# First attention's value products: softmax weights stationary, four heads in four column tiles

## The chip, the cores and the metric

The kernel runs on 1 core of one Trainium2 chip. The metric is the device time of one execution in microseconds; the time before is the median of 3 runs, 1287.91 us (1282.92 to 1290.34). Engines in the profile: PE is TensorE's matmul, PEld its weight load, DVE VectorE, ACT ScalarE, POOL GpSimd, SP SyncE, which issues most DMAs.

## The reference

Three parts follow one another, all in float32 (8 batches, 8 heads, 576 tokens, head size 64, 32 packing queries):

```python
def sm_attn(qq, kk, vv):
    s = scale * np.matmul(qq, kk.transpose(0, 1, 3, 2))
    s = s - np.max(s, axis=-1, keepdims=True)
    a = np.exp(s)
    a = a / (np.sum(a, axis=-1, keepdims=True) + 1e-09)
    return np.matmul(a, vv)
p_packed = sm_attn(p, k, v)          # first attention
out = sm_attn(q, p_packed, p_packed) # second attention
...
h = np.maximum(x @ w_in, 0.0)        # first MLP, 4608 x 512 x 2048
x = h * h @ w_out
...                                  # then a top-1 MoE of 8 experts, 512 x 1024 x 512
```

The change is in the last line of the first `sm_attn`: weights (32 x 576 per head) times values (576 x 64 per head).

## The kernel before, in words

**The first attention** works in 16 quads (four heads of one batch; `quads`, L282), each a generator `att1(i)` (L283) that is advanced by one step per iteration of the loop at L888. Its steps are:

1. scores: 32 packing queries of each head against the 576 keys, four matmuls into `s1` (L297); then the load of the K of quad i+3.
2. softmax: maximum (L308), exponential with the row's sum `sm` (L310), `sm` + 1e-9 and its reciprocal (L313, L314), and the scaling of all 128 x 576 weights by it on ScalarE (L315).
3. transposes: five, into PSUM tiles `ta` and `tb` (L320, L321), copied to `aT` on ScalarE (L322) and VectorE (L323). Rows of `aT` are now keys, columns are 4 heads x 32 queries.
4. value products `pq` (L329, L330): for each pair of heads (`g`) and each of five blocks of keys (four of 128, one of 64), the values of both heads (128 columns) are the stationary operand and 64 columns of `aT` the moving one. Each fp32 matmul is recorded as two instructions. The result has head size in rows; half of it is for the wrong head and is not used. Then the load of the V of quad i+4 (`load_v`), two copies of the wanted halves into `pp32` on VectorE (L334), and the split of `pp32` into a rounded part and a rest, `pphl` (L346 ScalarE, L347 GpSimd).

Quad i does step 1 in iteration i and step 4 in iteration i+3. In an iteration the oldest quad comes first, then from the newest to the next oldest (L891). The loop has 19 iterations.

**Beside it**, in the same loop: `conv_in` turns the first MLP's float64 weights into float32 halves in `wbt` (`convert`, L198: one ScalarE square, four VectorE operations, a ScalarE copy, a GpSimd difference); `att2(0)` is the second attention's first 384 tokens, from iteration `A20` on (L225, L896); and `pw_unit(bp, u)` (L352) multiplies the packed values of two batches (pair `bp`) with `w_in`, because the kernel applies the MLP's first weight to the packed values and not to the tokens. It makes three matmuls `ph` (L361), a copy `pws` (VectorE for odd pairs, L365; ScalarE for even ones, L367) in one of three buffers, and a write to DRAM (`pw_d`, L370). The table `PW` (L221 to L224) says which units are made in which iteration; those not made there follow in `others` (L914), with `conv_out`, which turns `w_out` and overwrites `wbt[:, u]` once all four pairs have used it. Only then does the MLP start (`layer1` L463, `layer2` L489), with the second attention's other tiles beside it, and at last the MoE (`group`, L768).

**Order.** Each engine has one queue and works in order. The program's order is a priority: a planner places the instructions of all engines by a simulated timeline and may interleave single matmuls of different steps. PSUM in this loop: `s1` has two tiles of two banks; `ta`, `tb`, `pq`, `pw`, `s2` and `ta2` share four banks in turn (`bank`, L256).

Of the kernel before, what the change touches and what calls it, by code (L numbers as in the profile page):

```python
# [20 lines left out]
P = 128  # L21
# [5 lines left out]
def tile_pack_attention_moe_moe2(  # L27
# [191 lines left out]
    w_out32 = w_out64.bitcast(I32).rearrange("r (f t) -> r f t", t=2)  # L219
    NU = 4 * HP  # L220
    PW = {9 + i: [(0, 2 * i), (0, 2 * i + 1)] for i in range(4)}  # L221
    PW |= {13 + i: [(1, 2 * i), (1, 2 * i + 1)] for i in range(6)}
    for i in range(3):
        PW[16 + i].append((2, i))  # L224
    A20 = 4  # L225
    PRI = 0
    a2T = {}

# [54 lines left out]
    def att1(i):  # L283
        b, qd = quads[i]
        pb = ptb[b % 2]
        if qd == 0:
            for j in range(2):
                nc.gpsimd.tensor_copy(
                    pb[j * D : (j + 1) * D, :, j * NPK : (j + 1) * NPK], pn[j * D : (j + 1) * D, b]
                )  # L290
        kT, vv, a, aT = kbuf[i % 3], vbuf[i % 4], abuf[i % 2], atbuf[i % 2]
        vt = vv[:, :16].rearrange("p (r h) d -> p r (h d)", h=4)
        vl = vv[:LAST, 16:].rearrange("p h d -> p (h d)")
        s1 = held["early"].tile([P, 2, 512], F32, tag="s1", name="s1", bufs=2)
        for hf in range(2):
            for pr in range(2):
                nc.tensor.matmul(  # L297
                    s1[pr * 64 : (pr + 1) * 64, hf, :HS],
                    pb[:, 2 * qd + pr, :],
                    kT[:, pr, hf * HS : (hf + 1) * HS],  # L300
                    start=True,
                    stop=True,
                )
        load_k(i + 3)
        yield
        mx = a_p.tile([P, 1], F32, tag="mx", name="mx")
        sm = a_p.tile([P, 1], F32, tag="sm", name="sm")
        nc.vector.tensor_reduce(out=mx, in_=s1[:, :, :HS], axis=AX.XY, op=ALU.max)  # L308
        nc.vector.tensor_scalar(out=mx, in0=mx, scalar1=-SCALE, scalar2=None, op0=ALU.mult)
        nc.scalar.activation(  # L310
            out=a.rearrange("p (h s) -> p h s", h=2), in_=s1[:, :, :HS], func=AF.Exp, bias=mx, scale=SCALE, accum_out=sm
        )
        nc.vector.tensor_scalar(out=sm, in0=sm, scalar1=EPS, scalar2=None, op0=ALU.add)  # L313
        nc.vector.reciprocal(out=sm, in_=sm)  # L314
        nc.scalar.activation(out=a, in_=a, func=AF.Copy, scale=sm)  # L315
        yield
        ta = bank("t", "ta")
        tb = bank("t", "tb")
        for r in range(4):
            nc.tensor.transpose(ta[:, r * P : (r + 1) * P], a[:, r * P : (r + 1) * P], ident)  # L320
        nc.tensor.transpose(tb[:LAST, :P], a[:, MAIN:S], ident)  # L321
        nc.scalar.activation(out=aT[:, 0:4, :].rearrange("p r n -> p (r n)"), in_=ta, func=AF.Copy)  # L322
        nc.vector.tensor_copy(aT[:LAST, 4, :], tb[:LAST, :P])  # L323
        yield
        pq = bank("t", "pq")
        for g in range(2):
            ds, ns = slice(2 * g * D, 2 * (g + 1) * D), slice(2 * g * NPK, 2 * (g + 1) * NPK)
            for r in range(4):
                nc.tensor.matmul(pq[:, ns], vt[:, r, ds], aT[:, r, ns], start=(r == 0), stop=False)  # L329
            nc.tensor.matmul(pq[:, ns], vl[:, ds], aT[:LAST, 4, ns], start=False, stop=True)  # L330
        load_v(i + 4)
        gs = slice(2 * qd, 2 * qd + 2)
        for j in range(2):
            nc.vector.tensor_copy(  # L334
                pp32[j * D : (j + 1) * D, b, gs, j * NPK : (j + 1) * NPK],
                pq[j * D : (j + 1) * D, :P].rearrange("p (g i n) -> p g i n", g=2, i=2)[:, :, j, :],
            )
        hl = pphl[:, b // 2].rearrange("p x g (b n) -> p x g b n", b=2)
        if b < 2:
            places = [(slice(2 * qd + i, 2 * qd + i + 1), (b + i) % 2) for i in range(2)]  # L340
        else:
            places = [(gs, b % 2)]
        for g, o in places:
            src = pp32[:, b, g, :]
            hi = hl[:, 0, g, o, :]
            nc.scalar.activation(out=hi, in_=src, func=AF.Copy)  # L346
            nc.gpsimd.tensor_tensor(out=hl[:, 1, g, o, :], in0=src, in1=hi.bitcast(F32), op=ALU.subtract)  # L347
        yield
# [536 lines left out]
    held["at"] = st3.enter_context(tc.tile_pool(name="at", bufs=1, side="left"))  # L885
    cv, co = [conv_in()], []
    runs, bg = [], []
    for i in range(len(quads) + 3):  # L888
        if i < len(quads):
            runs.append(att1(i))  # L890
        for r in (runs if i < 3 else runs[:1] + runs[:0:-1]):  # L891
            with tc.high_priority(offset=PRI):
                next(r)
        if i >= 3:
            runs.pop(0)
        if i == A20:  # L896
            bg = [att2(0)]
        pull(bg)
        pull(cv, 2)
        if i == 8:  # L900
            pull(cv, NU)
            held["head"] = const.tile([P, HEAD, 2, NPC, P], F32R, tag="head", name="head")
        for bp, u in PW.get(i, ()):
            pw_unit(bp, u)
# [156 lines left out]
```

## Time and profile before

| | us |
|---|---|
| median of 3 runs | 1287.91 |
| lowest, highest | 1282.92, 1290.34 |
| the profiled execution | 1283.14 |
| its span, first to last instruction | 1281.3 |
| TensorE busy in it | 1234.5 |
| VectorE busy | 810.7 |
| ScalarE busy | 600.7 |
| GpSimd busy | 323.9 |

The rows come from the one profiled execution. A line of a group gives line, engine, operation, what it writes and reads, its form (partitions x elements) and count, then busy time and mean ns of one, then the engine's idle time before it and what ended it. A line of the timeline gives start and length in us of instructions of one kind merged, with their count; the length runs to the end of the last one, and matmuls overlap the next one's start. The chain of waits is followed back from the stretch's last instruction to what released each step.

### The profile page before, as it was taken

How to read it: one execution, taken by the hardware profiler on the slowest of the kernel's cores; microseconds unless marked ns; L12 is line 12 of the kernel's file. 1: busy time of each engine (PE TensorE's matmuls, PEld its weight loads, DVE VectorE, ACT ScalarE, POOL GpSimd, SP SyncE). 2: the span in 40 equal slices, each digit the busy share in tenths (PEclk: the TensorE clock that was granted, in tenths of full speed). 3: DMA queues.
4: the chain of work that ended last, by engine and by line, in shares of the span. 5: the costliest groups of instructions: out<-in, count | busy, mean ns of one | idle time of the engine just before them, and what ended most of it. 6: DMA issues, size and time to landing. Idle time of an engine off the chain costs nothing.

```text
span 1281.3 us, 18377 instructions
## 1 busy us (share of the span) xinstructions
PE 1234.5 (96%) x6356; PEld 1029.2 (80%) x6356; DVE 810.7 (63%) x2040; ACT 600.7 (47%) x1209; POOL 323.9 (25%) x389
## 2 busy tenths in 40 slices
PE   7789999999999999999999999999999999999995
PEld 5567778788888888888888888878888888888884
DVE  4886866759676875767597396977644354354331
ACT  3575465555545565545654555642332343243220
POOL 4653456323101232012320033100221132022011
PEclk8798999999999999999999999989999999999998
DMA  9886665521211312012120122241442452353210
GB/s 343 285 293 197 181 172 174 165 76 51 67 43 29 89 50 76 32 35 76 50 84 17 34 68 83 90 152 51 173 152 99 146 181 95 121 198 111 87 67 36
DMA packets 74167, 145.06 MB, mean 113 GB/s; under 512 B 6608, under 2 KB 26192, under 8 KB 73936
## 3 DMA queue, kind: packets, MB, share of 16 engines
q1 hardware_dynamic: 68304, 124.62, 30.2%
q0 software_dynamic: 5760, 19.17, 4.5%
q8 instruction: 52, 0.85, 0.3%
q14 instruction: 51, 0.42, 0.1%
HBM read 109.92 MB, written 33.85 MB: 112 GB/s over the span
## 4 chain that ended last, share of the span: by engine, by line
PE 86%; DVE 5%; DMA 5%; ACT 2%; issue 1%; POOL 1%; SPq 0%; POOLq 0%; ACTq 0%; DVEq 0%
PE acc L493 28%; PE ph L473 16%; PE h L780 15%; PE o L802 15%; PE s L428 2%; PE pq L329 2%; PE pw L361 2%; DMA wraw<-in_moe_w 1%; PE tr L760 1%; PE s L297 1%; DMA wgb<-in_moe_w_out 1%; DMA rows<-in_moe_w_out 1%; PE pq L330 1%; PE ta L455 1%; PE ta L320 1%
## 5 line engine op out<-in xcount | busy, mean ns | idle before, releaser
L493 PE MATMUL acc<-wbt,ghl 128*128 128x512 f32 x1728 | 443.8, 399 | 0.0
L493 PEld LDWEIGHTS acc<-wbt,ghl 128*128 128x128 f32 x1728 | 316.5, 189 | 61.1 <-ACT ghl L484 0.4
L514 DVE SCALAR_TENSOR_TENSOR rows<-rows,wgb 128x512 f32<-128x512 f32 x288 | 217.2, 754 | 3.9
L780 PE MATMUL h<-xt,wbt 128*128 128x512 f32 x864 | 214.9, 399 | 0.0
L780 PEld LDWEIGHTS h<-xt,wbt 128*128 128x128 f32 x864 | 163.1, 189 | 39.0
L486 DVE TENSOR_TENSOR ghl<-r,ghl 128x384 fp32r<-128x384 f32 x176 | 108.0, 615 | 113.2 <-ACT ghl L484 112.5
L473 PE MATMUL ph<-a2T,ring 128*128 128x384 f32 (+1 forms) x840 | 145.2, 309 | 2.6 <-ACT ring L404 2.6
L484 ACT ACTIVATE ghl<-r 128x384 fp32r<-128x384 f32 x192 | 100.2, 522 | 98.4 <-PE acc L493 96.7
L473 PEld LDWEIGHTS ph<-a2T,ring 128*128 128x128 f32 x840 | 129.8, 190 | 10.8 <-ACT ring L404 3.0
L482 ACT ACTIVATE r<-ph 128x384 f32<-128x384 f32 x192 | 92.9, 486 | 89.1 <-PE ph L473 83.0
L791 DVE SCALAR_TENSOR_TENSOR ht<-h,ht 128x512 fp32r<-128x512 f32 x72 | 49.2, 688 | 117.9 <-ACT ht L790 117.9
L813 POOL DMA_INDIRECT out<-wgb,idx_s x36 | 36.5, 1013 | 342.5 <-DVE wgb L811 251.4
L473 PE MATMUL ph<-a2T,head 128*128 128x384 f32 (+1 forms) x696 | 118.9, 308 | 0.3 <-ACT r L482 0.3
L802 PE MATMUL o<-head,ht 128*128 128x512 f32 x432 | 113.6, 398 | 3.4 <-ACT ht L790 3.2
L790 ACT ACTIVATE ht<-h 128x512 fp32r<-128x512 f32 x72 | 42.5, 593 | 149.9 <-PE h L780 149.8
L802 PE MATMUL o<-ring,ht 128*128 128x512 f32 x432 | 111.6, 394 | 0.0
L473 PEld LDWEIGHTS ph<-a2T,head 128*128 128x128 f32 x696 | 106.1, 190 | 6.6 <-ACT r L482 0.4
L483 ACT ACTIVATE r<-r 128x384 f32<-128x384 f32 x192 | 100.0, 522 | 4.2
L802 PEld LDWEIGHTS o<-head,ht 128*128 128x128 f32 x432 | 81.0, 190 | 22.4 <-ACT ht L790 3.6
L405 POOL TENSOR_TENSOR ring<-praw,ring 128x256 fp32r<-128x256 f32 x62 | 52.0, 840 | 169.5 <-ACT ring L404 124.2
L802 PEld LDWEIGHTS o<-ring,ht 128*128 128x128 f32 x432 | 80.4, 188 | 16.9
L717 DVE TENSOR_TENSOR wbt<-wraw,wbt 128x1024 fp32r<-128x1024 f32 x36 | 44.1, 1225 | 47.7 <-ACT wbt L716 47.6
(210 smaller groups left out, 1470.1 us busy)
## 6 DMA issues: line engine op xcount, KB each, us to landing
wraw<-in_moe_w SPq DMA_DIRECT2D x72, 512.0 KB, 3.8
praw<-pw_d SPq DMA_DIRECT2D x56, 256.0 KB, 4.0
pw_d<-pws SPq DMA_DIRECT2D x48, 256.0 KB, 3.2
x_d<-rows SPq DMA_DIRECT2D x12, 792.0 KB, 4.1
qT<-in_q SPq DMA_DIRECT2D x36, 256.0 KB, 3.8
early<-in_v SPq DMA_DIRECT2D x16, 512.0 KB, 6.3
rows<-in_k SPq DMA_DIRECT2D x10, 576.0 KB, 6.4
wgb<-in_moe_w_out SPq DMA_DIRECT2D x11, 512.0 KB, 4.5
```

The source lines that it names most:

```text
L405: nc.gpsimd.tensor_tensor(out=t[:, 1], in0=raw, in1=t[:, 0].bitcast(F32), op=ALU.subtract)
L473: nc.tensor.matmul(ph[:, off : off + n], t[:, x, c, :], a[:, y, c, off : off + n], start=(i == 0), stop=(i == 3 * NPC - 1),)
L482: nc.scalar.activation(out=r, in_=ph, func=AF.Relu)
L483: nc.scalar.activation(out=r, in_=r, func=AF.Square)
L484: nc.scalar.activation(out=hl[:, 0], in_=r, func=AF.Copy)
L486: eng.tensor_tensor(out=hl[:, 1], in0=r, in1=hl[:, 0].bitcast(F32), op=ALU.subtract)
L493: nc.tensor.matmul(acc[t], hl[:, x, t * P : (t + 1) * P], wbt[:, f, y, :], start=(f == 0 and x == 0 and y == 0), stop=(f == NF - 1 and x = ...
L514: nc.vector.scalar_tensor_tensor(out=junk, in0=row[:, t, :DM], scalar=1.0, in1=wgb[:, e], op0=ALU.mult, op1=ALU.mult, accum_out=one)
L717: nc.vector.tensor_tensor(out=t[:, 1, :], in0=raw, in1=t[:, 0, :].bitcast(F32), op=ALU.subtract)
L780: nc.tensor.matmul(ph, half1[:, g % 2, c, x, f * P : (f + 1) * P], xs[c][:, y, :], start=(i == 0), stop=(i == 3 * NDC - 1),)
L791: nc.vector.scalar_tensor_tensor(out=h[:, 1, :], in0=ph, scalar=0.0, in1=h[:, 0, :].bitcast(F32), op0=ALU.max, op1=ALU.subtract)
L802: nc.tensor.matmul(po, hs[f][:, x, t * P : (t + 1) * P], second(f)[:, y, :], start=(i == 0), stop=(i == 3 * NFE - 1),)
```

## The change

Step 4 becomes two steps. In the first, `aT` is the stationary operand: for each block of keys and each head, the head's 32 columns are loaded in a column tile of their own (`tile_position=(0, h * 32)`), and the head's 64 value columns are the moving operand. The result `pv` has queries in rows (4 heads x 32) and head size in columns. It is copied to `pvs` on ScalarE with the scale `sm`, and the scaling of the weights in step 2 is gone. In the second, `pvs` is the stationary operand of two matmuls with columns of the identity as moving operand, which turn the result back and place the even and the odd heads in the two halves of the rows; the two copies into `pp32` read from there. A quad so ends in iteration i+4, the loop has 20 iterations, `sm` gets five buffers, `A20` is 5, and `PW` makes two more units of pair 1 in the loop and those of pair 2 one iteration later.

```diff
--- before.py
+++ after.py
@@ -219,10 +219,10 @@
     w_out32 = w_out64.bitcast(I32).rearrange("r (f t) -> r f t", t=2)
     NU = 4 * HP
     PW = {9 + i: [(0, 2 * i), (0, 2 * i + 1)] for i in range(4)}
-    PW |= {13 + i: [(1, 2 * i), (1, 2 * i + 1)] for i in range(6)}
+    PW |= {13 + i: [(1, 2 * i), (1, 2 * i + 1)] for i in range(7)}
     for i in range(3):
-        PW[16 + i].append((2, i))
-    A20 = 4
+        PW[17 + i].append((2, i))
+    A20 = 5
     PRI = 0
     a2T = {}
 
@@ -304,7 +304,7 @@
         load_k(i + 3)
         yield
         mx = a_p.tile([P, 1], F32, tag="mx", name="mx")
-        sm = a_p.tile([P, 1], F32, tag="sm", name="sm")
+        sm = a_p.tile([P, 1], F32, tag="sm", name="sm", bufs=5)
         nc.vector.tensor_reduce(out=mx, in_=s1[:, :, :HS], axis=AX.XY, op=ALU.max)
         nc.vector.tensor_scalar(out=mx, in0=mx, scalar1=-SCALE, scalar2=None, op0=ALU.mult)
         nc.scalar.activation(
@@ -312,7 +312,6 @@
         )
         nc.vector.tensor_scalar(out=sm, in0=sm, scalar1=EPS, scalar2=None, op0=ALU.add)
         nc.vector.reciprocal(out=sm, in_=sm)
-        nc.scalar.activation(out=a, in_=a, func=AF.Copy, scale=sm)
         yield
         ta = bank("t", "ta")
         tb = bank("t", "tb")
@@ -322,18 +321,31 @@
         nc.scalar.activation(out=aT[:, 0:4, :].rearrange("p r n -> p (r n)"), in_=ta, func=AF.Copy)
         nc.vector.tensor_copy(aT[:LAST, 4, :], tb[:LAST, :P])
         yield
+        pv = bank("t", "pv")
+        for r in range(5):
+            k = P if r < 4 else LAST
+            for h in range(4):
+                ns = slice(h * NPK, (h + 1) * NPK)
+                nc.tensor.matmul(
+                    pv[ns, :D], aT[:k, r, ns], (vt[:, r] if r < 4 else vl)[:, h * D : (h + 1) * D],
+                    start=(r == 0), stop=(r == 4), tile_position=(0, h * NPK),
+                )
+        load_v(i + 4)
+        pvs = a_p.tile([P, D], F32, tag="pvs", name="pvs", bufs=2)
+        nc.scalar.activation(out=pvs, in_=pv[:, :D], func=AF.Copy, scale=sm)
+        yield
+        gs = slice(2 * qd, 2 * qd + 2)
         pq = bank("t", "pq")
-        for g in range(2):
-            ds, ns = slice(2 * g * D, 2 * (g + 1) * D), slice(2 * g * NPK, 2 * (g + 1) * NPK)
-            for r in range(4):
-                nc.tensor.matmul(pq[:, ns], vt[:, r, ds], aT[:, r, ns], start=(r == 0), stop=False)
-            nc.tensor.matmul(pq[:, ns], vl[:, ds], aT[:LAST, 4, ns], start=False, stop=True)
-        load_v(i + 4)
-        gs = slice(2 * qd, 2 * qd + 2)
+        heads = ident.rearrange("p (g i n) -> p i g n", g=2, i=2)
+        for j in range(2):
+            nc.tensor.matmul(
+                pq[j * D : (j + 1) * D, : 2 * NPK].rearrange("p (g n) -> p g n", g=2), pvs, heads[:, j],
+                start=True, stop=True,
+            )
         for j in range(2):
             nc.vector.tensor_copy(
                 pp32[j * D : (j + 1) * D, b, gs, j * NPK : (j + 1) * NPK],
-                pq[j * D : (j + 1) * D, :P].rearrange("p (g i n) -> p g i n", g=2, i=2)[:, :, j, :],
+                pq[j * D : (j + 1) * D, : 2 * NPK].rearrange("p (g n) -> p g n", g=2),
             )
         hl = pphl[:, b // 2].rearrange("p x g (b n) -> p x g b n", b=2)
         if b < 2:
@@ -885,13 +897,13 @@
     held["at"] = st3.enter_context(tc.tile_pool(name="at", bufs=1, side="left"))
     cv, co = [conv_in()], []
     runs, bg = [], []
-    for i in range(len(quads) + 3):
+    for i in range(len(quads) + 4):
         if i < len(quads):
             runs.append(att1(i))
-        for r in (runs if i < 3 else runs[:1] + runs[:0:-1]):
+        for r in (runs if i < 4 else runs[:1] + runs[:0:-1]):
             with tc.high_priority(offset=PRI):
                 next(r)
-        if i >= 3:
+        if i >= 4:
             runs.pop(0)
         if i == A20:
             bg = [att2(0)]
```

## Rows read from the trace of the kernel before

**Rows 1.** Page, section 1: busy time of each engine over the whole span

```profile
PE 1234.5 (96%) x6356; PEld 1029.2 (80%) x6356; DVE 810.7 (63%) x2040; ACT 600.7 (47%) x1209; POOL 323.9 (25%) x389
```

**Rows 2.** Busy time by stretch (stretch, length, engines, clock, DMA)

```profile
core 0: us, PE busy (x) PEld busy (x) DVE busy (x) ACT busy (x) POOL busy (x), PEclk, DMA share, GB/s
5.00:43.00 38.00, 28.49 (x136) 19.15 (x136) 24.68 (x57) 18.25 (x36) 17.87 (x33) 0.76 0.99 347
43.00:73.00 30.00, 28.73 (x161) 20.18 (x162) 24.97 (x65) 18.98 (x43) 19.66 (x21) 0.85 0.88 299
73.00:105.00 32.00, 26.45 (x160) 19.40 (x159) 26.06 (x57) 20.91 (x41) 19.64 (x18) 0.89 0.70 234
105.00:136.00 31.00, 30.26 (x177) 23.92 (x177) 17.88 (x43) 15.04 (x31) 5.54 (x8) 0.94 0.62 211
136.00:235.00 99.00, 91.09 (x440) 74.62 (x438) 68.46 (x96) 58.81 (x120) 57.55 (x49) 0.98 0.64 191
240.00:760.00 520.00, 520.00 (x2918) 453.85 (x2917) 371.56 (x1090) 282.56 (x629) 108.79 (x130) 1.00 0.19 54
```

**Rows 3.** Chain of waits by line, in the four stretches 5:43, 43:73, 73:105, 105:136

```profile
by line: PE pq L329 15.0%; PE s L297 11.5%; DMA wgb<-in_k 10.7%; PE ta L320 7.8%; POOL wbt L216 6.7%; DVE stage L212 6.4%; DVE stage L209 6.0%; issue 5.7%; PE pq L330 5.2%; DVE wgb L206 4.4%; ACT L310 3.4%; ACT wbt L215 3.3%; ACT atbuf L322
by line: PE pq L329 32.3%; PE s L297 29.8%; PE pq L330 10.5%; PE ta L320 9.2%; PE pw L361 5.3%; ACT atbuf L322 3.6%; PE s L428 2.8%; PE ta L455 2.8%; PE tb L321 2.3%; ACT pws L367 2.0%; ACT wgb L202 1.8%; issue 0.5%
by line: DMA pw_d<-pws 15.0%; POOL head L377 9.3%; issue 6.9%; DVE wgb L212 6.8%; DVE stage L206 5.3%; DVE wgb L209 5.2%; DVE wgb L206 5.2%; DVE mx L308 4.7%; DVE stage L212 4.4%; POOL wbt L216 3.9%; DVE stage L209 3.8%; DVE sm L446 3.7%; D
by line: PE pw L361 38.5%; PE pq L329 32.1%; PE pq L330 11.7%; PE s L297 6.8%; PE ta L320 6.2%; PE tb L321 3.1%; ACT pws L367 2.0%; issue 0.3%; ACTq L367 0.1%
```

**Rows 4.** TensorE in order of time, one quad at full clock (start, length, work)

```profile
58.98 1.19 PE L297 MATMUL s<-rows,ptb 128*64 128x288 f32 x8
60.10 1.10 PE L329 MATMUL pq<-atbuf,early 128*128 128x64 f32 x8
61.14 0.43 PE L330 MATMUL pq<-atbuf,early 64*128 64x64 f32 x2
61.50 1.10 PE L329 MATMUL pq<-atbuf,early 128*128 128x64 f32 x8
62.53 0.43 PE L330 MATMUL pq<-atbuf,early 64*128 64x64 f32 x2
62.90 0.66 PE L320 MATMUL ta<-ident,abuf 128*128 128x128 f32 x4
```

**Rows 5.** Second attention's scores in 64-column tiles: two runs in time, then their group

```profile
360.10 0.69 PE L428 MATMUL s<-pp,qT 128*64 128x64 f32 x12
...
515.26 0.68 PE L428 MATMUL s<-pp,qT 128*64 128x64 f32 x8
...
L428 PE MATMUL s<-pp,qT 128*64 128x64 f32 x64 | 4.8, 230 | 0.0
```

**Rows 6.** TensorE in order of time, products mixed with scores

```profile
64.24 0.66 PE L329 MATMUL pq<-atbuf,early 128*128 128x64 f32 x4 [0.58 <-ACT atbuf L322]
...
67.45 0.43 PE L330 MATMUL pq<-atbuf,early 64*128 64x64 f32 x2
67.81 1.10 PE L329 MATMUL pq<-atbuf,early 128*128 128x64 f32 x8
```

**Rows 7.** TensorE in order of time, shortest matmuls of the trace

```profile
322.57 0.29 PE L566 MATMUL pc<-s,ones 128*128 128x8 f16 x6
```

**Rows 8.** ScalarE groups of the first 136 us, by form

```profile
L315 ACT ACTIVATE abuf<-abuf,sm 128x576 f32<-128x576 f32 x16 | 12.2, 768 | 4.8 <-DVE sm L314 2.6 <-DVE mx L309 2.1
L346 ACT ACTIVATE pphl<-pp 128x64 fp32r<-128x64 f32 x8 | 1.7, 249 | 4.6 <-DVE pp L334 4.6
```

**Rows 9.** Copies of pw, 105:136; SyncE's waits there; landing of their DMA

```profile
L365 DVE COPY pws<-pw 128x512 f32<-128x512 f32 x12 | 8.1, 688 | 3.4 <-PE pw L361 3.3
...
SPq L370 <- DVE pws L365: 15.0, 11, 3.6
...
DMA to landing us min/median/max: 2.3/3.2/6.5
```

## The prediction

> **What bounds the kernel now.** I read the page's busy times first: TensorE is busy for 96% of the span, more than any other engine [rows 1]. A busy share is an average, so the table by stretch comes next. The change sits in the first attention, which runs from about 5 to 135 us. There TensorE is busy for 28.49 of 38 us, 28.73 of 30, 26.45 of 32 and 30.26 of 31 in four stretches, and VectorE is close behind in the second and third (24.97 of 30, 26.06 of 32). From 240 to 760 us TensorE fills its time completely [rows 2]. That part is mostly the first MLP, and the change doesn't touch it, so what the first attention gains can reach the end only as an earlier start of everything behind it.
>
> The chain of waits tells which of these busy times decides [rows 3]. In 43:73 the value products (pq, L329 and L330) hold 32.3 + 10.5 = 42.8% of the chain, 12.8 us. In 105:136 they hold 32.1 + 11.7 = 43.8%, 13.6 us. In 5:43 they hold 15.0 + 5.2 = 20.2%, 7.7 us, beside weight conversions on VectorE and GpSimd and a load of K. In 73:105 they are not among the entries: VectorE's conversions (L206 to L212), GpSimd and a write of pw are. So there are two stretches in which cheaper products pay at once, and one between them in which they don't.
>
> **The products, per quad.** One quad (four heads of one batch) issues 20 product instructions: 10 matmuls of fp32, each recorded twice. At full clock they start at 60.10 and the next work starts at 62.90: 2.80 us [rows 4]. Eight instructions of 128 rows take 1.04 us to the next start, two of 64 rows take 0.36 us. If a step costs s and a change of the array's shape c, then 8s + c = 1.04 and 2s + c = 0.36: s = 0.113 us, c = 0.133 us. A quad is 20 steps (2.27) and four changes (0.53).
>
> The new code issues 20 matmuls (40 instructions) with 32 columns of weights, in four column tiles, and 2 matmuls (4 instructions) to turn the result back. The nearest rows are the second attention's scores, with 64 columns of weights and 64 moving columns [rows 5]. Eight in one tile last 0.68 us; less the mean length of one (0.23) that is seven steps of 0.064 us. Where two tiles were at work, twelve lasted 0.69 us: four more at no price, so tiles do run beside each other. The same shows in the first attention's scores, two tiles of 288 columns.
> - If four tiles run together, ten steps decide: 10 x 0.064 = 0.64 us. The turn takes two steps, 0.13 us. Changes of shape: into 32 columns, into 64 rows, out again, into 64 columns for the turn, four of 0.133: 0.53. Sum 1.30 us, 1.50 less than now.
> - If nothing overlaps, 44 steps and four changes are 2.82 + 0.53 = 3.35 us, 0.55 more than now.
>
> I take 1.30, since the two-tile row shows overlap. The point between is (2.80 - 0.53 - 0.13)/40 = 0.053 us per instruction.
>
> **What of it lies on the path.** 43:73 has four quads, now 12.8 us on the chain: 4 x 1.30 = 5.2, so up to 7.6 us less. 105:136 has five: 13.6 - 6.5 = 7.1 us less.
> - In 105:136 VectorE is busy for 17.88 of 31 us and ScalarE for 15.04 [rows 2], so they can follow. Next in line are the buffers of pw: three, each held through its copy (0.69 us) and its write (3.2 us to landing), 3.9 us, or 1.3 us per unit [rows 9]. The changed loop makes 17 units in this part (14 of pair 1, 3 of pair 2), so 22 us at the least, and 31 - 7.1 is 24 us. SyncE already waits 15.0 us for these copies. That is near enough to cost something: I take 6.0 of 7.1, with 4 and 7.1 as ends.
> - In 43:73 VectorE's 24.97 us is a floor that leaves 5.0 at most, and the following 73:105 is held by VectorE, GpSimd and a DMA. An earlier start there is worth only what VectorE has free. I take 2.0, with 0 and 5.0 as ends.
> - 5:43 and 73:105: I take nothing; 0 to 2 together, for the cases in which a product ends last in a short wait.
>
> **The rest of the edits.** The scaling of the softmax on ScalarE goes (16 x 0.768 = 12.2 us) and a copy of 128x64 with the scale comes; the nearest row is 0.249 us [rows 8], so 16 x 0.25 = 4.0. ScalarE isn't the bound in any stretch [rows 2], and I cost its 8.2 us at nothing. The transposes no longer wait for the reciprocal, which stands in VectorE's queue behind conversions. ScalarE waited 2.6 + 2.1 us for it before L315 [rows 8]; that wait moves to the new copy, which has a whole iteration. If that cover is missing, the turn waits and all of TensorE's queue behind it: scores, transposes, pw; the price is the same 4.7 us at most.
>
> The fifth step makes the loop one iteration longer. The last quad's path to pw of pair 3 gains a copy and a turn (0.25 + 0.13 + 0.13 = 0.5 us) and what it waits; three pw units (nine instructions) lie beside it. I take +0.5, 0 to 2. The two pw units that move into the loop cost six instructions there and save two copies of 0.69 us on VectorE behind it, where VectorE is busy for 68.46 of 99 us: these cancel. The V loads are issued behind the products as before, and no sooner than TensorE releases them; K is loaded at the same place. The second attention's first tile starts one iteration later (A20); its first use, the first layer of the MLP, comes behind the loop and is on no chain here [rows 3]. In PSUM the four banks of the early pool serve one more tile per iteration; a bank that is still to be copied stops TensorE's queue. It's a part of the lower ends above.
>
> **Sum.** -6.0 - 2.0 + 0.5 = -7.5 us. The profiled execution took 1283.14 us with a span of 1281.3, so it would become 1275.6. It lies 4.8 us under the median of the runs, 1287.91 (1282.92 to 1290.34), from which the same sum is 1280.4. I forecast the middle, 1278. The likeliest case by itself runs from -3 to -12 us.
>
> **Rivals.**
> - *All of it counts.* The 14.7 us of both stretches and up to 2 more, from the middle of the two times before (1285.5): 1269 to 1271. For it: the chain gives the products 26.4 us in these two stretches. Against it: VectorE at 83% in 43:73.
> - *Swallowed.* The array is free sooner, and TensorE waits for VectorE's conversions, a PSUM bank or a pw buffer instead: within 2 us of 1285.5. For it: 73:105 is such a stretch already.
> - *Not what it says: the tiles don't run together.* 9 quads on the path x 0.55 = +5 us, 1290.5. Against it: twelve instructions in 0.69 us are (0.69 - 0.23)/11 = 0.042 us a start [rows 5], under the point of 0.053, and six matmuls of 8 columns in 0.29 us, of which the last alone is 0.17, are 0.025 [rows 7]; both are short runs, and 40 may come slower. Here the Trainium skill speaks against the change: its page "TensorE: Matmul & The Clock Gate", in "Wait — 56ns, not 53.3ns?", has the sequencer spend about 62 ns on each MATMUL when the hardware's own decoder is off, and by that 40 of them are 2.48 us and nothing is gained. The starts of [rows 5, 7] don't agree with it.
> - *Slower: the planner mixes the tiles with whole-array work.* It orders single matmuls, and did so at 64.24: ten product and eight score instructions took 3.57 us to 67.81 [rows 6], where 1.40 and 1.12 would be their own [rows 4], so 1.05 us were lost. Now a quad has 20 matmuls to put something between, each time with two changes (0.27 us) and without its neighbour tiles. From six such breaks on (1.50/0.27) a quad gains nothing; with 20, each matmul alone, it takes 20 x (2 x 0.064 + 0.27) = 8.0 us, 5.2 more than now. Of the nine quads on the path two in that state undo what seven gain (7 x 1.50 = 10.5); with three the sum is 15.6 - 9.0 = +6.6 us, 1292. Against it: the quad of [rows 4] runs unbroken.
>
> **How the numbers follow.** Chances: forecast 0.52, all of it 0.15, swallowed 0.13, tiles not together 0.08, mixed 0.12. Within 0.5%, 6.4 us, a measurement of this kernel can't tell a change from none. Of the forecast's own range about two thirds lie beyond it: 0.36, with 0.15 from the first rival: faster 0.51. Same: 0.16 + 0.13 + 0.06 = 0.35. Slower: 0.02 + 0.12 = 0.14. The range reaches from 1266, where all of it counts, to 1292, which takes in the swallowed case from the higher runs, the serial tiles and the mild end of the mixed case.
>
> **What would show it.** In the changed profile: the products' 40 instructions of a quad in under 1.2 us from first to last start, in 105:136 the iterations about 1.3 us shorter, the products' share of the chain there about half of 43.8%, pw higher, and the last quad's results ready by about 128 us. Wrong it is if product instructions of 32 columns start 0.05 us or more apart, if whole-array matmuls stand between them in most quads, if the chain of 43:73 turns to VectorE with the same length, or if the granted clock of 105:136 falls well below 0.94.

## The result and the profile after

The changed kernel takes 1298.07 us, the median of 5 executions (1293.13 to 1299.58), beside 1287.54 us for the kernel before on the same chip. The ratio is 1.0085, with a 95% interval of 1.0062 to 1.0108: it is slower by 0.6 to 1.1%, some 11 us. The forecast was 1278, the range 1266 to 1292. Of the kernel before 97 more executions were made beside the experiments; two of them, of 1299.8 us, count as a slower state. The median of the other 95 is 1286.0 us, and differences below are taken from it where no other is named. A ratio with its interval is the one on record for that comparison; it is not exactly the quotient of the two medians.

The profiled execution of the change took 1299.58 us, with a span of 1297.8, 16.5 us over that of before. The first rows are the busy times of the page and the table by stretch; they answer to [rows 1] and [rows 2].

```profile
PE 1230.7 (95%) x6740; PEld 1009.5 (78%) x6740; DVE 820.0 (63%) x2040; ACT 593.6 (46%) x1209; POOL 319.1 (25%) x389
```

```profile
core 0: us, PE busy (x) PEld busy (x) DVE busy (x) ACT busy (x) POOL busy (x), PEclk, DMA share, GB/s
5.00:43.00 38.00, 24.38 (x156) 10.90 (x156) 19.11 (x45) 13.49 (x29) 14.83 (x31) 0.69 0.94 332
43.00:73.00 30.00, 25.00 (x246) 16.14 (x247) 23.10 (x58) 13.95 (x35) 12.44 (x14) 0.61 0.76 260
73.00:105.00 32.00, 25.14 (x264) 14.32 (x260) 30.12 (x64) 16.91 (x38) 15.73 (x17) 0.82 0.77 255
105.00:136.00 31.00, 23.14 (x231) 13.79 (x232) 21.63 (x42) 18.35 (x39) 15.93 (x13) 0.73 0.53 179
136.00:235.00 99.00, 88.29 (x470) 69.72 (x470) 70.60 (x94) 54.06 (x110) 49.60 (x42) 0.97 0.53 165
240.00:760.00 520.00, 518.38 (x2903) 451.67 (x2902) 362.20 (x1063) 282.00 (x631) 108.78 (x131) 1.00 0.21 62
```

TensorE does have less to do: it is busy for 23.14 of 31 us in 105:136, where it was for 30.26. But the granted clock is lower in every stretch up to 136: 0.69, 0.61, 0.82 and 0.73, against 0.76, 0.85, 0.89 and 0.94. And VectorE's work has moved to a later time: 19.11 us in 5:43 for 24.68 before, and 30.12 of 32 in 73:105 for 26.06.

The chain by line, in 43:73 and in 105:136, answers to [rows 3]:

```profile
by line: PE s L440 14.6%; PE pv L329 13.3%; PE ta L319 9.6%; POOL wbt L216 9.1%; PE pq L341 8.4%; PE s L297 5.4%; DVE sm L458 4.1%; DVE stage L212 4.0%; POOL e L460 3.4%; POOL pphl L359 3.4%; POOL ptb L288 3.3%; issue 2.9%; PE tb L320 2.6%;
...
by line: DMA wgb<-in_moe_w_out 19.1%; issue 12.7%; PE pw L373 10.2%; ACT head L388 8.1%; PE pv L329 6.8%; DVE pws L377 6.1%; DVE rows L212 5.7%; DVE wgb L209 4.4%; DVE rows L209 3.6%; PE pq L341 3.5%; ACT pws L379 3.5%; DVE wgb L206 2.8%; P
```

In 43:73 products and turn (pv, pq) hold 21.7% for 42.8% before. In 105:136 they hold 10.3% for 43.8%; the largest other entries are a load (19.1%), time in which the chain's engine waited for nothing shown (12.7%), the matmuls and copies of pw, and conversions (L206 to L212), which before were at home in 73:105. The chain has gone over to work that comes late.

A quad at full clock, in order of time, answers to [rows 4] and [rows 5]:

```profile
123.63 0.90 PE L329 MATMUL pv<-early,atbuf 128*32 128x64 f32 x40
124.46 1.67 PE L373 MATMUL pw<-wbt,pphl 128*128 128x512 f32 x6
126.06 0.33 PE L341 MATMUL pq<-ident,pvs 128*64 128x64 f32 x2
126.32 0.33 PE L319 MATMUL ta<-ident,abuf 128*128 128x128 f32 x1
126.58 0.33 PE L341 MATMUL pq<-ident,pvs 128*64 128x64 f32 x2
```

Forty product instructions hold TensorE for 124.46 - 123.63 = 0.83 us, the change of shape included, where twenty held it for 2.80. The part that the change is about does what it says.

So where do the 16.5 us come from? Four points in time tell it for each kernel: conv_in's last difference (the 16th start of L216; in the kernels without changed lines above it the number is the same), the last copy into pp (the end of the first attention), and conv_out's first and last difference (the 17th and 32nd start of L216). Far behind the loop nothing is gained or lost for long: the second attention's 20th load of q, at 449 us, is 18.05 us later than before, and so is its 34th, at 715.

| profiled execution | conv_in ends | last pp | conv_out starts | conv_out ends | span | median |
|---|---|---|---|---|---|---|
| before | 97.6 | 134.3 | 137.1 | 225.7 | 1281.3 | 1286.0 |
| change | 110.2 | 146.6 | 152.8 | 245.4 | 1297.8 | 1298.07 |
| e3 no fifth step | 99.7 | 136.2 | 138.3 | 227.2 | 1282.6 | 1284.51 |
| e2 units back | 108.3 | 145.1 | 147.2 | 235.1 | 1287.5 | 1290.35 |
| e14 units back, A20 = 4 | 104.8 | 140.8 | 142.9 | 230.3 | 1285.2 | 1289.71 |
| e18 units back, catching up | 106.3 | 144.7 | 147.0 | 235.5 | 1290.8 | 1292.50 |
| e16 no fifth step, A20 = 5 | 110.6 | 148.3 | 150.3 | 239.1 | 1292.7 | 1295.04 |
| e17 the same, catching up | 104.3 | 139.4 | 141.4 | 229.3 | 1283.8 | 1287.45 |
| e5 before, units moved | 100.9 | 138.5 | 143.6 | 237.1 | 1289.2 | 1288.36 |
| e6 before, fifth step | 98.8 | 147.0 | 149.2 | 238.3 | 1292.8 | 1303.70 |
| e13 the same, A20 = 4 | 94.2 | 141.3 | 143.5 | 234.0 | 1288.5 | 1285.25 |
| e1 before, fifth step, units moved | 96.3 | 143.9 | 148.3 | 242.5 | 1294.8 | 1298.65 |

By it the change loses 12.3 us up to the last pp, 3.4 more before conv_out starts, 4.0 while conv_out runs, and gets 3.2 back later. The 12.3 us are there when conv_in ends, which is 12.6 us late: from there to the last pp it takes 36.4 us, before 36.7. One execution is not the median: e6's profiled one took 1294.67 us, 9 under its median, e13's took 1290.35, 5 over. In some sets the times of single executions go with the mean granted clock, in others not: of e13's ten the fastest, 1280.42 us, had 0.977 and the slowest, 1295.24, had 0.965 (correlation -0.94), but over the 95 of before the correlation is -0.44, and in the five sets of which they consist it lies between -0.01 and -0.83.

### The profile page after: what moved, and what is told of

It is laid out like the page before. It is cut to its first block, busy times and chain, and to the rows that moved or that the text cites. A ratio compares the mean times of both kernels' runs of the same rounds, so it can differ in the third digit from the quotient of the medians.

```text
span 1297.8 us, 19140 instructions
## 1 busy us (share of the span) xinstructions
PE 1230.7 (95%) x6740; PEld 1009.5 (78%) x6740; DVE 820.0 (63%) x2040; ACT 593.6 (46%) x1209; POOL 319.1 (25%) x389
## 4 chain that ended last, share of the span: by engine, by line
PE 82%; DVE 8%; DMA 4%; issue 2%; ACT 2%; POOL 1%; SPq 0%; POOLq 0%; ACTq 0%; DVEq 0%
PE acc L505 28%; PE ph L485 15%; PE h L792 15%; PE o L814 15%; PE s L440 2%; PE pw L373 2%; PE tr L772 1%; DVE rows L526 1%; PE s L297 1%; PE pv L329 1%; DMA pw_d<-pws 1%; DMA wgb<-in_moe_w_gate 1%; DMA wgb<-in_moe_w_out 1%; DMA wgb<-in_k 1%; PE ta L319 1%
## 5 line engine op out<-in xcount | busy, mean ns | idle before, releaser
L825 POOL DMA_INDIRECT out<-wgb,idx_s x36 | 36.5, 1013 | 341.0 <-DVE wgb L823 251.4
```

## The experiments

All were timed beside the kernel before on the same chip. In e13 and e14 the second attention's first tile of 128 tokens reads the packed values of half the heads of its batch before they are written; the amount of work is unchanged, but the unit lacks a wait there that it has in the others. In e4, e11 and e12 the products of four key blocks are computed and then computed again, with the same result. A diff shows the lines in question; `...` stands for what is left out.

**First set: the change taken apart.**

*e1*, the kernel before with the step, the two moved units and A20 = 5, but the old products:

```diff
         yield
+        yield
         pq = bank("t", "pq")
 ...                    # PW, A20 and the loop's length as in the change
```

> The old products (10 whole-array matmuls, weights scaled on ScalarE) in the new schedule: a fifth step that is empty, 20 iterations, A20 and PW as changed. Theory A (the longer loop and its moved pw units cost the time): 8 to 14 us slower than before, like the changed kernel. Theory B (the products' new form lets TensorE fall idle and to the lower clock): within 4 us of before, granted clock of 43:73 near 0.85.

1298.65 us, ratio 1.0111 (1.0079 to 1.0143), as theory A had it: a loss of the same size is there without a single tiled product.

*e2*, the change with the table of units of before:

```diff
-    PW |= {13 + i: ... for i in range(7)}
+    PW |= {13 + i: ... for i in range(6)}
-        PW[17 + i].append((2, i))
+        PW[16 + i].append((2, i))
```

> The changed kernel with the table PW of before: two pair-1 units fewer in the loop, pair 2 one iteration earlier. Theory A: 3 to 6 us faster than the changed kernel (1291 to 1295), since each unit holds a pws buffer for its write ahead of the MLP's start. Theory B: no change, 1297 to 1299.

1290.35, ratio 1.0028 (1.0009 to 1.0046): 7.7 us of the change's loss are the table of units, a little more than theory A's 3 to 6. The table moves two things, the two units of pair 1 and, by one iteration, the three of pair 2; no run has the second alone.

*e3*, e2 without the fifth step (copy and turn in one step, 19 iterations, A20 = 4):

```diff
         nc.scalar.activation(out=pvs, in_=pv[:, :D], func=AF.Copy, scale=sm)
-        yield
 ...                    # A20 and the loop's length as before
```

> The new products, with the turn in the same step as the tiles: 19 iterations, A20 and PW of before. Theory A: 5 us or more faster than before (1275 to 1282), the gain that was forecast. Theory B: slower than before by 4 us or more, with the granted clock of 43:73 still near 0.6.

1284.51, ratio 0.9987 (0.9975 to 0.9999), between the two theories: the tiled products by themselves win 1.5 us, and the other 5.8 us go with the fifth step and its A20. Its chain in 105:136 and TensorE's waits there show why so little is won:

```profile
by line: DMA wgb<-in_moe_w_out 21.4%; DMA pw_d<-pws 20.5%; PE pw L372 17.9%; PE s L297 6.1%; DVE wgb L212 6.0%; PE pv L329 5.6%; DVE pws L376 4.9%; issue 3.5%; PE pq L340 3.0%; DVE wgb L209 2.6%; DVE wgb L206 2.2%; ACT pws L378 1.9%; DVE pp
```

```profile
PE pq L340 <- ACT pvs L335: 4.7, 5, 2.2
```

Products and turn hold 8.6% there, the writes of pw and a load 42%, and TensorE stands for 4.7 us before the turn until the scaled copy is made. The chain is the "swallowed" rival's.

*e4*, the change with its tiles' products twice, to see whether TensorE's time or its clock is at fault:

```diff
-        for r in range(5):
+        for n, r in enumerate((0, 1, 2, 3, 0, 1, 2, 3, 4)):
 ...                    # each sum is closed after the fourth and the last block
```

> The changed kernel with the four blocks of 128 keys multiplied twice (the first result is overwritten by the second): 32 product instructions more per quad, 0.5 to 0.6 us of TensorE at full clock. Theory A: 3 to 8 us slower than the changed kernel where TensorE ends last. Theory B: not slower than the changed kernel, or faster, with a higher granted clock in 43:73 and 105:136, because the array is kept busy.

1301.55, ratio 1.0121 (1.0104 to 1.0139): 3.5 us over the change, near the least that theory A named, and with the higher clock of theory B. More work raised the granted clock of 43:73 from 0.61 to 1.00, and conv_in ended at 100.9 instead of 110.2; the last pp stayed at 146.4:

```profile
43.00:73.00 30.00, 24.32 (x491) 15.79 (x490) 29.46 (x70) 18.16 (x43) 16.66 (x19) 1.00 0.91 315
```

**Second set: each schedule edit alone.**

*e5*, the kernel before and `PW[18] += [(1, 12), (1, 13)]`:

> The kernel before with one line more: the two pair-1 units (1,12) and (1,13) are issued in the attention loop's iteration 18 instead of after the loop; the products stay as they were and no step is added. Theory (the two units are half of the loss: their copies pws and the DMA writes behind them come when the three pws buffers are already the late thing, and hold up the MLP's first units): 1290 to 1294, about 3 to 7 us over the kernel before. Rival, the prediction's own step (six instructions in the loop against two copies saved after it, which cancel): within 1.5 us of the kernel before, 1285 to 1288.

1288.36, ratio 1.0019 (0.9987 to 1.0050): by the time neither is excluded. Its profile shows what the theory supposes: conv_out starts 5.1 us after the last pp where it started 2.8 after it, and runs for 93.5 us where it ran for 88.6.

*e6*, e1 with the table of units of before (`range(6)`, `PW[16 + i]`):

> The kernel before with a fifth, empty step in each quad's work, one iteration more, the second attention's first unit one iteration later, and the projection units where they stood (the earlier run with the empty step had the two units moved as well: 1298.65). Theory (the two units cost 7 to 8 us wherever they are moved, and the additional step by itself a few): 1289 to 1293. Rival (the additional step costs only together with the tiled products, so the earlier run's loss was the units alone): within 1.5 us of the kernel before, 1285 to 1288; then the last pp copy is back near 134 us. Second rival (the step alone was the loss, and the units are nothing without the tiled products): 1296 or more.

1303.70, ratio 1.0134 (1.0081 to 1.0187): the second rival. With the old products the step, with its A20, costs 17.7 us alone (by the interval 10 to 24), and moving the units on top of it (e1) costs nothing more. So the edits' prices don't add.

*e7* and *e8* leave `PW[16 + i].append((2, i))` out, in e3 and in the kernel before:

> The tiled products without the additional step (1284.51, ratio 0.9987) and without the three pair-2 units in the loop, which are then made after it together with pair 3. Theory (in that kernel the end of the first attention waits for pws buffers and their writes, so that the products' gain is swallowed there): last pp copy 2 to 4 us sooner than its 136.2, whole kernel 1280 to 1283. Rival (the units only move behind the loop and take the same time there): 1284 to 1286. Other side (they cost more behind the loop, where the MLP waits for them): 1287 or more.

> The kernel before without the three pair-2 units in the loop. Theory (the end of attention is bound by pws there too, behind the products): 1 to 3 us sooner at the last pp copy, whole kernel 1283 to 1287, so that less is won than with the tiled products. Rival: the products are the bound at the end of attention there and the units fill gaps, so that moving them out costs 1 to 4 us: 1288 to 1291.

e7 1286.60 (1.0008; 0.9986 to 1.0030), e8 1289.48 (1.0019; 0.9994 to 1.0044), in its rival's range, though the interval takes in no change. In e7 the last pp came at 130.8, 5.4 us sooner, as the theory said, but the end did not: the units take their time behind the loop.

**Third set: the units' place against the step.** *e9* is e6, *e10* is e2, *e12* is e10 with the tiles twice, all with every unit of the loop one iteration later; *e11* is e3 with the tiles twice.

```diff
-    PW = {9 + i: ...}      # pair 0
+    PW = {10 + i: ...}
-    PW |= {13 + i: ...}    # pair 1, then (2, i) at 17 + i
+    PW |= {14 + i: ...}
```

> The empty fifth step with the old products (1303.70 with the projection units where they stood), and now every projection unit of the loop one iteration later, so that units and products stand to each other as in the kernel before. Theory (the step costs because the units of pair 0, which wait for the end of conv_in, stand one iteration ahead of the products then, so that seven quads' products are left behind that wait instead of six: one iteration of some 5 us, and TensorE at 1.2 GHz over more of it): six quads are left again, the last pp copy is at 133 to 138, and the time is 1285 to 1290. Rival (a fifth step costs an iteration at the end wherever the units stand, since fill and drain are one longer): last pp copy 139 or later, 1291 to 1300.

> The whole change with the projection units one iteration later and pair 1 of six iterations again, as in the kernel before (the run with six iterations and no shift: 1290.35). Theory (two separate losses: the units' place, which this takes away, and conv_in, whose last unit comes 11 us late because TensorE runs at 1.2 GHz over most of the first 73 us): conv_in's last unit is still at 105 to 110, the last pp copy 3 to 6 us sooner than 145.1, 1285 to 1288. Rival (the place of the units explains conv_in's lateness too): conv_in back at 97 to 100, 1280 to 1283. Rival (the place is nothing with the tiled products): 1289 to 1292.

> The tiled products without the fifth step (1284.51), with 32 product instructions more in each quad (the first four tiles' products are computed twice and the sum restarted, so the result's work is the same and only TensorE has more to do). Theory (TensorE is not the bound there and its granted clock of 0.71 between 43 and 73 us is: more instructions raise the clock and cost nothing): clock 43 to 73 at 0.9 or more, conv_in's last unit at 96 to 99, 1281 to 1285. Rival (TensorE's own time is the bound): 16 times 0.8 us at most is added, of which the part behind conv_in, six quads, counts: 4 to 5 us, 1288 to 1290.

> The change with the units one iteration later, pair 1 of six iterations, and the tiles' products twice: both losses of the theory taken away. Theory: conv_in's last unit at 97 to 102, six quads left behind it, last pp copy at 135 to 140, 1283 to 1288. Rival (the fifth step costs by itself, about an iteration of 5 us): last pp copy 142 or later, 1290 or more.

e9 1302.50 (1.0102; 1.0036 to 1.0169), e10 1301.42 (1.0135; 1.0114 to 1.0155), e11 1292.48 (1.0033; 1.0006 to 1.0061), e12 1307.56 (1.0145; 1.0082 to 1.0209). By the time none of the four theories came out. The one that the step costs because the units stand ahead of the products fell: e10's last pp came 4.1 us sooner than e2's (141.0), and the kernel still got 11 us slower. e11 shows the clock again (0.94 in 43:73 for e3's 0.71, conv_in at 96.4) and that it isn't enough: its time rose by 6 us by the ratios and 8 by the medians, its rival's side: behind conv_in TensorE's own work seems to count (last pp at 141.3 for 136.2). In e9, e10 and e12 conv_out runs for 92.3 to 95.4 us, in the kernels with the two moved units for 91.8 to 94.2; with the table of before it is 87.4 to 90.4, but for e15 below (94.1).

**Fourth set: the step against A20.** A20 says in which iteration the second attention's first unit begins; the fifth step had brought 5 for 4. *e13* is e6 and *e14* is e2 with `A20 = 4`, *e16* is e3 with `A20 = 5`; *e15* is e3 with the tiled products in the transposes' step and the turn alone in the last.

> The empty fifth step with the old products (1303.70), but the second attention's first unit starts in iteration 4 as in the kernel before, not 5. Theory (it is the step that costs: each quad's products come one iteration later, out of a stretch where TensorE has slack into the one after conv_in where it is the bound): last pp copy at 142 to 148 again, 1293 or more. Rival (the one iteration by which the second attention is put off is the loss): last pp copy back at 133 to 138, 1285 to 1288.

> The whole change with the projection units where they stood (1290.35) and the second attention's first unit in iteration 4 instead of 5. Theory (the step costs, not A20): last pp copy at 142 to 147, 1288 to 1293. Rival (A20 is what makes conv_in late there, by putting VectorE's work for the second attention ahead of conv_in's fifth unit at 38 to 54 us): conv_in's last unit at 97 to 101, last pp copy at 134 to 137, 1283 to 1286.

> Four steps as in the kernel before, the tiled products in the transposes' step and the turn alone in the last one (the run without the fifth step had products and turn together in the last one: 1284.51). Theory (a quad's products one iteration sooner than in the change: TensorE has done one quad more when pair 0's units wait for conv_in): last pp copy at 131 to 137, 1281 to 1285. Rival (the products then wait behind the copies of the transposes made just before, 1 to 2 us in each quad, and that counts behind conv_in): 1286 to 1291.

> The tiled products without the fifth step (1284.51), the second attention's first unit in iteration 5 instead of 4. Theory (A20 by itself is worth little): 1283 to 1287. Rival (A20 is the loss of the step): last pp copy 140 or later, 1289 or more.

e13 1285.25 (1.0001; 0.9974 to 1.0029): with the old products the step itself costs nothing, and A20 all of it; the rival was right on the time. Its last pp, at 141.3, isn't back at 133 to 138, and the wait that e13 lacks may have a part in it. e16 1295.04 (1.0077; 1.0059 to 1.0096): A20 alone costs 10.5 us with the tiled products too. e14 1289.71 (1.0035; 1.0017 to 1.0053): with tiled products and fifth step A20 = 4 gives back only 0.6. e15 1301.10 (1.0128; 1.0105 to 1.0150), over theory and rival: the worst of the three places tried for the products.

**Fifth set: the late start or the late end.** *e17* is e16, *e18* is e2, each with two of the second attention's nine parts pulled in iteration 5, so that it ends in the iteration in which it did before:

```diff
-        pull(bg)
+        pull(bg, 2 if i == A20 else 1)
```

> The tiled products without the fifth step, the second attention's first unit from iteration 5 (1295.04 with that), but with two of its nine parts pulled in iteration 5, so that it ends in iteration 12 again as in the kernel before. Theory (the late start costs at its end, where its last parts then stand beside the projection units in iterations 10 to 13 and hold up VectorE and conv_in): back at 1284 to 1288, conv_in's last unit at 97 to 102. Rival (it costs at its start, where VectorE and TensorE are left without that work and the clock falls): 1292 or more.

> The whole change with the projection units where they stood (1290.35) and two of the second attention's parts pulled in iteration 5. Theory (as for the run without the fifth step): conv_in's last unit at 99 to 104 instead of 108.3, 1284 to 1288. Rival (the start is what counts, or the fifth step itself): within 2 us of 1290.35.

e17 1287.45 (1.0016; 1.0002 to 1.0030): 7.6 of the 10.5 us are back, so it is not the late start. Every part but the first is moved up there, so the run doesn't tell the last part from those between. e18 1292.50 (1.0051; 1.0035 to 1.0067): nothing is back, so with fifth step and tiled products something else holds. VectorE's differences into a2T, three in each kernel, show the end of that unit: first and last start, in e3, e16, e17 and, one line further down, in the change.

```profile
L470 DVE TENSOR_TENSOR a2T<-ta,a2T x3: 410/416/424, 49.4 to 94.9; 128x256 fp32r<-128x256 f32 x3
```

```profile
L470 DVE TENSOR_TENSOR a2T<-ta,a2T x3: 404/423/423, 51.5 to 122.5; 128x256 fp32r<-128x256 f32 x3
```

```profile
L470 DVE TENSOR_TENSOR a2T<-ta,a2T x3: 419/424/425, 45.4 to 89.9; 128x256 fp32r<-128x256 f32 x3
```

```profile
L471 DVE TENSOR_TENSOR a2T<-ta,a2T x3: 399/410/424, 66.4 to 119.3; 128x256 fp32r<-128x256 f32 x3
```

In e3 and e17 the last is made at 95 and 90 us, before conv_in's end (99.7 and 104.3); in e16 at 122.5 and in the change at 119.3, behind it (110.6 and 110.2). Between lies the point at which the whole loop stands: pair 0's units write `head`, which takes the memory of conv_in's `stage`. In the change, TensorE and the first of the copies into `head`:

```profile
108.07 1.65 PE L373 MATMUL pw<-wbt,pphl 128*128 128x512 f32 x3 [5.02 <-ACT pws L379]
```

```profile
L388 ACT ACTIVATE head<-pws x6: 612/627/630, 105.1 to 111.6; 64x512 fp32r<-64x512 f32 x6
```

The first copy into `head` starts at 105.1, just after conv_in's last operation on VectorE's `stage` (L209, 103.9 to 105.0), and TensorE has stood still for 5.02 us when it goes on at 108.07. TensorE runs at half clock there, 0.50 (1.2 GHz) in every 5 us from 95 to 120. But little of e16's price lies behind that wait: from conv_in's end to the last pp it takes 37.7 us and e3 36.5, while conv_in itself ends 10.9 us later than in e3.

## Why the prediction was wrong

**Products per quad: right.** 1.30 us was reckoned; 0.83 for the products and 0.22 for the turn (83.57 to 83.79) were found at full clock. The forty start within 0.68 us, about ten steps of 0.064; that is 0.0175 us for each instruction, far under the point of 0.053. What was over-rated seem to be the changes of shape. The rival "tiles don't run together" is out. The Trainium skill, page "TensorE: Matmul & The Clock Gate", section "Wait — 56ns, not 53.3ns?", has about 62 ns for each MATMUL where hardware decode is off; at 0.0175 us a start this trace doesn't show that price.

**What lies on the path: mis-sized.** -8.0 us was the sum of the two terms -6.0 and -2.0; the products alone, e3, gave -1.5. The 6.0 of 105:136 assumed that pw's buffers would take little of it. In e3 the writes of pw, a load and the wait for the scaled copy hold that stretch, and from conv_in's end to the last pp its profile has 36.5 us where the kernel before has 36.7. Nor do the 2.0 of 43:73 show: conv_in ends at 99.7 for 97.6. That was the rival "swallowed", at 0.13. Removing TensorE's work gains 1.5 us while adding some (e11) costs 8.0.

**"The second attention's first tile starts one iteration later (A20); its first use ... is on no chain here": failed.** Its first use is indeed far behind, but the unit itself is work in the queues that conv_in needs, and its time was put at nothing. e16 prices it at 10.5 us, e13 against e6 at 18.4 by the medians (4.3 by the profiled executions), and e17 gives most of e16's back by moving up all but the first part. How it costs is not shown. In e16's profile 10.9 of the 12.1 us up to the last pp are lost before conv_in ends. There two quads' scores stand in pieces between transposes, from 58.3 and from 80.7 us, the second at half clock, and VectorE waits 5.2 us for them; e3 has one such quad, at full clock (82.0), and e17 has none in as many pieces. In the change this price doesn't show by itself (e14, e18); conv_in is late there in any case, as told below.

**"The two pw units that move into the loop ... cancel": failed.** From e2 to the change they cost, together with pair 2's later place, 7.7 us, in the profiled executions 10.3. 4.1 of these lie before conv_out starts: it comes 2.1 us after the last pp in e2, 6.2 in the change, and TensorE waits 2.9 us for a copy of pw there. 4.7 lie in conv_out, and one place has more than that: from its 11th to its 12th difference pass 6.7 us in e2 and 12.7 in the change. There ScalarE waits for a load, and TensorE for pw:

```profile
ACT wgb L202 <- DMA wgb<-in_moe_w_out: 6.8, 1, 6.8
```

```profile
216.46 1.16 PE L373 MATMUL pw<-wbt,pphl 128*128 128x512 f32 x3 [3.54 <-DVE pws L377]
```

The load isn't slow but late: it is issued at 215.11, when VectorE has read its buffer for the last time (L209, to 215.09), and VectorE had waited 4.3 us for GpSimd just before. All kernels in which the two units or the whole table moved (the change, e1, e4, e5, e9, e10, e12) have a gap of 12.5 to 12.7 us there, e7 and e8, without pair 2, one of 11.2, and all that have the table of before, but one, 6.7 to 7.2; e15, with that table, has 12.6. e5 moves the two units alone and has it too. As e15 makes the same units as before, the number of instructions isn't what decides; that the order of issue is, is likely but not shown.

**"The fifth step ... +0.5": failed, and its way is not wholly settled.** With A20 it costs 5.8 us from e3 to e2; neither A20 = 4 nor catching up takes that away. The profiles put the loss at one place. conv_in's fifth difference comes 8.9 us later in e2 than in e3 (52.2 and 43.3; 53.8 in the change, 42.1 before), its last one 8.6, the last pp 8.9. From the fifth difference on the four kernels run alike: 55.5 to 56.4 us to conv_in's end, 36.4 to 36.8 from there to the last pp. At that place the planner has mixed the scores of one quad with transposes, TensorE at half clock, in the change:

```profile
36.70 0.47 PE L319 MATMUL ta<-ident,abuf 128*128 128x128 f32 x1 [8.97 <-DMA wgb<-in_k]
37.10 1.22 PE L297 MATMUL s<-rows,ptb 128*64 128x288 f32 x2
38.26 0.48 PE L319 MATMUL ta<-ident,abuf 128*128 128x128 f32 x1
38.66 1.22 PE L297 MATMUL s<-rows,ptb 128*64 128x288 f32 x2
...
43.04 0.76 DVE L308 TENSOR_REDUCE mx<-s 128x1 f32<-128x576 f32 x1 [4.84 <-PE s L297]
```

and before, also at half clock:

```profile
35.58 2.19 PE L297 MATMUL s<-rows,ptb 128*64 128x288 f32 x8 [3.88 <-ACT abuf L310]
```

Alone between transposes a score matmul in one of two tiles takes 1.16 us to the next start; eight instructions in a row, four matmuls, take 2.19. VectorE waits 4.84 us for the mixed scores, and conv_in's next operations stand behind them in its queue. The seven kernels with tiled products and fifth step (the change, e2, e4, e10, e12, e14, e18) and e15 have this mix at 34 to 38 us, and 13.1 to 17.8 us pass in them from conv_in's fourth difference to its fifth; in the twelve others it is 6.4 to 12.3. So it is the rival "the planner mixes", at 0.12 and priced at +6.6 in its mild form, but by scores first, and not by the products alone. No run took this mix away and left the step and the tiled products, so it is argued, not shown. That the clock takes part is shown by e4, which keeps the mix and has conv_in 9 us sooner.

The products are broken too: of the 16 quads' products, 9 are broken by other work in the change, 9 in e2, e14 and e18, and 11 in e15; where products and turn stand in one last step, it is 2 (e3, e7) or 1 (e16, e17). But in the kernel before it was 11, with 25 breaks; the prediction's "the quad of [rows 4] runs unbroken" took one of the other five. What a break of the tiled products costs is to be read where one quad is broken once by three instructions of pw:

```profile
133.79 0.88 PE L329 MATMUL pv<-early,atbuf 128*32 128x64 f32 x34
134.60 0.96 PE L373 MATMUL pw<-wbt,pphl 128*128 128x512 f32 x3
135.50 0.31 PE L329 MATMUL pv<-early,atbuf 64*32 64x64 f32 x6
135.74 0.96 PE L373 MATMUL pw<-wbt,pphl 128*128 128x512 f32 x3
```

From 133.79 to 135.74 it is 1.95 us; 0.83 are the unbroken products' own, 0.80 half of the six pw instructions at 124.46, and 0.32 remain. The change has 18 such breaks, 6 of them behind conv_in's end, where they come to 1.9 us; e3 has none there and isn't faster in that part (36.5 us for 36.4). So behind conv_in the products' breaks cost nothing that the end shows. Ahead of it they may add to the lateness: from 43.3 to 47.2 one quad's products are mixed with the second attention's scores, and VectorE waits 2.2 us for these.

**The sum along one path** is -1.5 (products, e3) + 5.8 (step with A20, e2) + 7.7 (units) = +12.0, the measured 12.1 by medians. Along another, with the old products to the last, it is +17.7 (e6), -5.1 (e1) and -0.6. Both sums reach the total by construction, since each term is the difference of two kernels; what they show is that the division depends on the order. Of the list of what would prove the forecast wrong, the lower clock came true, and so did mixing in most quads, which the kernel before had as well.

The best version tried is e3, 0.13% faster than the kernel before; its interval, 0.01 to 0.25%, only just leaves out no gain at all.

## What to carry to other kernels

When a step is added to a software pipeline, price what the longer pipeline drags along, by asking of each background job which wait it is issued behind now and which one then: here the job that slid by one iteration cost 10.5 us with the new products and 18.4 with the old, and the faster matmuls gave 1.5. Where a planner orders single matmuls, look after the change for groups that it has newly mixed, not only among the matmuls that were changed, and for the engine that waits for them: here it was VectorE, for scores. Find the first point in time at which the kernels part, and look there. Try each schedule edit that comes with a change by itself before reading the change's own worth from the total.

## What the hardware showed that was not expected

Forty fp32 product instructions in four 32-column tiles start within 0.68 us at full clock and within 1.14 at half, and at full clock the next work, of another shape, starts 0.15 us after the last of them (0.83 less 0.68). Less work on TensorE can bring a lower clock for all that is left: with 32 instructions more in each quad the granted clock of 43:73 rose from 0.61 to 1.00 (e4), from 0.71 to 0.94 (e11) and from 0.63 (e10) to 0.94 (e12); all three kernels got slower even so.
